# The written order of 1233 steps, the loads' order and the places of the tiles, all drawn up anew

## The chip, the cores and the metric

The program runs on one core of a Trainium2 chip. The metric is device time in microseconds (us): 275.06 us before, the median of three runs (273.14, 275.06 and 277.61).

## What is computed

A column-normalised attention, whose output is the input of a soft mixture of experts; B, N, C are 4, 5056, 256 and there are 32 slots.

```python
def _attn_ref(q, k, v, tau):                 # per batch
    qn = q / (np.linalg.norm(q, axis=1, keepdims=True) + 1e-06)
    kn = k / (np.linalg.norm(k, axis=1, keepdims=True) + 1e-06)
    s = kn.transpose(0, 2, 1) @ qn / tau     # 256 x 256
    a = softmax(s)
    return v @ a

def _moe_ref(x, phi, w1, w2):                # x: all rows of all batches
    logits = x @ phi                         # 20224 x 32
    slot_input = softmax(logits, axis 0).T @ x
    slot_out = per expert: np.maximum(slot_input[e] @ w1[e], 0.0) @ w2[e]
    return softmax(logits, axis 1) @ slot_out
```

## The kernel before

**Tiles.** Inputs come in tiles of 1 MiB (128 partitions by 2048 fp32), each one DMA on SP's queue. There are 40 tiles q0 to q39 (ten for each batch; each holds four pieces of q and k side by side), 20 tiles v0 to v19, nine tiles x4 to x12 (v transposed by the host), eight w1 tiles and eight w2 tiles. The output leaves in 21 stores. All these tiles and the large intermediates live in 23 places of 1 MiB. `SLOTS` says which place each takes; a load into a place waits for the last reader of the tile that was there before. `BANKS` does the same for the eight PSUM banks.

**Stages.** For each q tile: `cast` (L356, ScalarE) makes the high half of a split pair, `low` (L360, GpSimd, 117 of them) the low half, `square` (L370, ScalarE) the squares, `add` (L388, VectorE) sums them, and `score` (L408, TensorE) multiplies each piece into S, either the split pair or the raw fp32 tile. After the ten tiles of a batch comes a chain that ends in M, the attention matrix times phi: `att_cols` (L444, TensorE), `att_rn` (L449, VectorE), `att_pow` (L454, GpSimd, a square root), `att_norm` (L458 ScalarE, L459 VectorE), `att_row` (L471, TensorE), `att_scale`, `att_exp`, `att_turn`, `att_phi` (L511). With M, each v tile gives `logits` (L566, TensorE; needs v transposed: from an x tile, or by `turn`, L546, and a copy, L551), then exponentials, and `gather` (L666, TensorE). After the last, `gather(19)`, come `finish` steps, the experts (`up` L810, `flip_h` L828, `down` L843, `o_fold` L859), and 29 `out_mul` steps (L878 for half blocks of 512 rows by 128 columns of output, L893 for whole blocks). Each `out_mul` is copied out of PSUM by four `out_evict` (L906, ScalarE and VectorE in turn) and stored by SP (L911). On the side, GpSimd does `c_sub` and `c_mul` (L764, L779) for the softmax over the slots.

**What sets the order.** `plan` lists 1233 steps by name. `run` executes them in the order of `ORDER`, a list of their numbers, and so every engine, SP's queue included, gets its own steps in the order in which they stand there; each engine works in order, and semaphores make it wait for data and for places. No planner runs: the order, the places and the banks are written out.

Of the kernel before, what the change touches and what calls it, by code (L numbers as in the profile page):

```python
# [58 lines left out]
    901, 10, 9, 0, 11, 1, 903, 34, 33, 12, 42, 17, 20, 35, 900, 902, 30, 21, 22, 899, 897, 898, 2, 15, 26,  # L59
    904, 27, 19, 8, 18, 41, 39, 29, 14, 16, 45, 46, 50, 36, 23, 28, 51, 24, 38, 905, 13, 58, 57, 907, 54, 5,  # L60
    43, 47, 7, 32, 82, 48, 56, 6, 906, 81, 912, 61, 60, 59, 70, 908, 909, 83, 914, 84, 87, 65, 89, 44, 69,
    31, 145, 77, 91, 85, 25, 49, 147, 92, 93, 78, 90, 76, 64, 3, 72, 71, 148, 73, 62, 75, 74, 80, 910, 95,
    149, 96, 86, 94, 911, 105, 106, 63, 4, 146, 37, 66, 55, 99, 40, 97, 110, 111, 88, 917, 79, 155, 156, 53,
    102, 173, 915, 120, 174, 52, 98, 100, 113, 124, 107, 150, 157, 895, 913, 115, 104, 68, 158, 109, 151,
    112, 118, 131, 67, 132, 133, 108, 103, 176, 177, 153, 134, 117, 183, 101, 135, 121, 821, 119, 916, 114,
    126, 140, 152, 154, 141, 123, 825, 826, 942, 896, 918, 125, 217, 175, 221, 189, 116, 122, 824, 823, 127,
    185, 184, 130, 143, 142, 827, 828, 216, 829, 128, 830, 834, 211, 136, 178, 220, 219, 222, 203, 187, 223,
    137, 160, 225, 129, 197, 186, 831, 224, 201, 215, 159, 182, 190, 194, 572, 227, 568, 198, 163, 205, 231,
    919, 162, 920, 213, 161, 832, 835, 169, 179, 239, 228, 208, 921, 171, 924, 244, 164, 922, 196, 207, 180,
    138, 237, 218, 139, 168, 170, 566, 570, 204, 212, 236, 167, 248, 188, 202, 206, 172, 144, 191, 192, 247,  # L70
    837, 229, 571, 226, 166, 210, 238, 245, 567, 230, 243, 569, 234, 255, 214, 278, 292, 235, 181, 258, 254,
    193, 232, 165, 320, 264, 200, 249, 233, 310, 199, 314, 312, 250, 246, 209, 256, 240, 573, 836, 284, 833,
    241, 925, 242, 923, 306, 252, 195, 311, 838, 253, 282, 324, 298, 263, 259, 260, 313, 265, 322, 839, 840,
    262, 290, 316, 317, 842, 841, 941, 319, 285, 251, 268, 257, 560, 554, 321, 266, 315, 926, 940, 542, 548,
    561, 318, 327, 293, 555, 546, 270, 543, 843, 305, 549, 288, 844, 291, 556, 289, 335, 960, 271, 558, 544,
    269, 279, 547, 261, 557, 545, 574, 286, 577, 302, 340, 550, 927, 929, 845, 559, 562, 267, 273, 272, 846,
    275, 576, 353, 551, 294, 326, 552, 323, 564, 930, 303, 344, 345, 347, 283, 848, 334, 847, 575, 296, 280,
    281, 354, 352, 356, 578, 277, 579, 553, 852, 600, 849, 332, 359, 304, 853, 339, 850, 563, 338, 357, 365,
    287, 928, 299, 297, 307, 348, 355, 346, 580, 276, 565, 274, 343, 341, 342, 943, 588, 362, 854, 962, 376,
    590, 295, 591, 934, 360, 361, 301, 300, 368, 581, 372, 364, 350, 851, 931, 380, 383, 381, 385, 384, 363,  # L80
    367, 371, 856, 349, 589, 333, 582, 366, 351, 594, 358, 592, 369, 330, 331, 370, 584, 933, 585, 593, 382,
    595, 374, 325, 586, 603, 596, 602, 599, 386, 411, 329, 985, 309, 393, 857, 328, 986, 855, 440, 377, 858,
    583, 587, 932, 961, 373, 396, 378, 375, 387, 390, 598, 604, 388, 379, 389, 445, 400, 401, 337, 336, 308,
    618, 601, 397, 417, 937, 402, 439, 605, 861, 597, 425, 620, 862, 863, 444, 391, 392, 621, 606, 965, 419,
    944, 501, 607, 608, 442, 407, 394, 622, 859, 426, 508, 418, 408, 430, 623, 453, 452, 443, 404, 946, 963,
    403, 626, 624, 619, 611, 628, 629, 433, 860, 625, 438, 612, 455, 964, 441, 938, 448, 409, 459, 460, 641,
    645, 630, 609, 613, 434, 631, 451, 395, 450, 412, 644, 424, 428, 436, 627, 864, 866, 429, 935, 865, 515,
    632, 520, 635, 432, 431, 614, 420, 449, 945, 870, 437, 633, 947, 954, 519, 410, 415, 528, 468, 527, 471,
    514, 615, 634, 647, 642, 987, 646, 399, 637, 500, 516, 638, 639, 867, 416, 616, 871, 447, 643, 427, 446,
    640, 953, 507, 617, 699, 705, 936, 456, 648, 414, 422, 467, 649, 706, 509, 988, 505, 464, 523, 504, 518,  # L90
    650, 872, 398, 868, 423, 435, 406, 513, 512, 454, 458, 457, 869, 526, 405, 651, 461, 522, 478, 477, 463,
    484, 958, 966, 939, 486, 493, 494, 476, 701, 691, 465, 873, 700, 783, 692, 487, 495, 967, 874, 413, 875,
    703, 876, 968, 704, 462, 499, 466, 517, 525, 421, 777, 469, 610, 636, 956, 778, 502, 689, 473, 488, 503,
    654, 652, 479, 492, 491, 530, 702, 529, 779, 532, 510, 781, 524, 668, 782, 531, 784, 521, 664, 780, 996,
    672, 496, 666, 667, 511, 485, 538, 742, 949, 539, 534, 470, 675, 506, 690, 738, 533, 541, 540, 948, 955,
    475, 489, 481, 743, 687, 670, 674, 676, 536, 535, 653, 673, 740, 669, 688, 537, 665, 472, 693, 483, 741,
    671, 694, 879, 880, 881, 490, 677, 678, 959, 655, 882, 679, 989, 656, 657, 480, 732, 730, 739, 497, 731,
    658, 733, 728, 729, 660, 498, 661, 474, 482, 795, 789, 878, 659, 883, 884, 877, 888, 885, 680, 997, 990,
    950, 796, 993, 992, 998, 957, 951, 726, 793, 727, 707, 662, 695, 886, 790, 681, 683, 684, 952, 889, 891,
    999, 890, 794, 709, 697, 711, 887, 744, 752, 753, 892, 893, 682, 745, 663, 1000, 894, 754, 756, 755,  # L100
    791, 712, 792, 710, 713, 696, 750, 751, 734, 708, 698, 736, 757, 785, 788, 746, 748, 758, 714, 715, 760,
    716, 747, 717, 721, 797, 762, 799, 763, 735, 759, 764, 769, 765, 685, 718, 719, 787, 801, 1001, 995,
    770, 800, 766, 773, 686, 767, 771, 772, 720, 749, 768, 786, 802, 803, 722, 798, 774, 775, 723, 969, 724,
    804, 805, 976, 806, 761, 807, 1007, 725, 810, 811, 808, 809, 776, 812, 814, 815, 813, 816, 819, 975,
    973, 974, 820, 737, 817, 1008, 1018, 818, 1009, 1019, 1037, 991, 1010, 972, 970, 971, 1029, 1030, 1048,
    1011, 1049, 978, 977, 980, 1038, 1056, 994, 1002, 1031, 1032, 1057, 1050, 1012, 1058, 1039, 1051, 1020,
    1059, 1033, 1034, 1005, 1003, 1040, 1006, 1021, 1004, 1035, 1036, 979, 1041, 1042, 1043, 1044, 1045,
    1022, 982, 984, 981, 1023, 1016, 1013, 1046, 1047, 1087, 1090, 1015, 1088, 1127, 1089, 1128, 1132, 1133,
    1091, 1135, 1129, 1131, 983, 1134, 1136, 1077, 1130, 1080, 1081, 1067, 1069, 1220, 1071, 1078, 1082,
    1083, 1052, 1053, 1084, 1085, 1070, 1079, 1072, 1054, 1055, 1060, 1061, 1086, 1076, 1068, 1073, 1027,  # L110
    1074, 1122, 1124, 1075, 1126, 1062, 1063, 1064, 1117, 1065, 1119, 1121, 1218, 1125, 1123, 1118, 1120,
    1066, 1107, 1109, 1108, 1214, 1212, 1112, 1116, 1111, 1110, 1115, 1114, 1113, 1162, 1165, 1163, 1216,
    1164, 1221, 1177, 1166, 1202, 1179, 1180, 1205, 1178, 1204, 1203, 1223, 1102, 1181, 1104, 1014, 1142,
    1144, 1146, 1206, 1226, 1106, 1105, 1103, 1145, 1147, 1151, 1148, 1150, 1215, 1025, 1137, 1140, 1143,
    1026, 1139, 1141, 1092, 1094, 1024, 1138, 1217, 1095, 1231, 1096, 1167, 1171, 1168, 1170, 1169, 1197,
    1198, 1200, 1199, 1201, 1157, 1230, 1149, 1160, 1187, 1188, 1224, 1189, 1190, 1191, 1161, 1192, 1193,
    1017, 1028, 1196, 1195, 1159, 1172, 1174, 1194, 1175, 1228, 1176, 1173, 1225, 822, 1182, 1229, 1183,
    1184, 1207, 1208, 1210, 1211, 1158, 1097, 1222, 1099, 1100, 1098, 1209, 1152, 1155, 1153, 1154, 1156,
    1219, 1232, 1093, 1186, 1101, 1185, 1227, 1213,
]  # L120
SLOTS = {
    "q0": 6, "q1": 0, "q2": 7, "q3": 3, "q4": 11, "q5": 12, "q6": 15, "q7": 13, "q8": 17, "q9": 18,
    "q10": 20, "q11": 21, "q12": 16, "q13": 0, "q14": 19, "q15": 12, "q16": 10, "q17": 22, "q18": 16,
# [1019 lines left out]
```

## Time and profile before

| | |
|---|---|
| median of three runs | 275.06 us (273.14 to 277.61) |
| the profiled execution's own time | 276.03 us |
| its span, first to last instruction | 274.3 us |
| moved by DMA | 109.73 MB, of it 88.38 MB read and 20.97 MB written by the kernel's own loads and stores |
| busy: TensorE (PE), VectorE, ScalarE, GpSimd (POOL) | 250.7, 207.8, 206.9, 170.2 us |
| mean granted TensorE clock | 0.96 |

How to read it: busy shares are shares of the span. The page cuts the span into 40 slices of 6.86 us and gives a digit (tenths busy) for each engine and the GB/s moved. "Idle before" is the time an engine stood still before an instruction, with what ended it.

### The profile page before, as it was taken

How to read it: one execution, taken by the hardware profiler on the slowest of the kernel's cores; microseconds unless marked ns; L12 is line 12 of the kernel's file. 1: busy time of each engine (PE TensorE's matmuls, PEld its weight loads, DVE VectorE, ACT ScalarE, POOL GpSimd, SP SyncE). 2: the span in 40 equal slices, each digit the busy share in tenths (PEclk: the TensorE clock that was granted, in tenths of full speed). 3: DMA queues.
4: the chain of work that ended last, by engine and by line, in shares of the span. 5: the costliest groups of instructions: out<-in, count | busy, mean ns of one | idle time of the engine just before them, and what ended most of it. 6: DMA issues, size and time to landing. Idle time of an engine off the chain costs nothing.

```text
span 274.3 us, 5939 instructions
## 1 busy us (share of the span) xinstructions
PE 250.7 (91%) x2272; PEld 197.2 (72%) x2272; DVE 207.8 (76%) x416; ACT 206.9 (75%) x325; POOL 170.2 (62%) x135
## 2 busy tenths in 40 slices
PE   5799999999999999999989999999999899999800
PEld 5688888888898778776758977976545767767500
DVE  1068998599998999889979987799957756965410
ACT  3999999899999999999998793665837445653500
POOL 1776999999999989999998797903054300000000
PEclk9999999999999999999999999999999999996755
DMA  7999999999998999999999999999999997999995
GB/s 276 417 421 418 424 422 420 410 424 422 412 418 337 375 362 361 424 422 419 418 412 421 415 384 403 424 423 421 417 421 418 394 415 326 415 416 421 409 405 244
DMA packets 16013, 109.73 MB, mean 400 GB/s; under 512 B 1905, under 2 KB 1905, under 8 KB 3569
## 3 DMA queue, kind: packets, MB, share of 16 engines
q1 hardware_dynamic: 15984, 109.36, 97.5%
q8 instruction: 18, 0.29, 0.4%
q14 instruction: 11, 0.08, 0.1%
HBM read 88.38 MB, written 20.97 MB: 399 GB/s over the span
## 4 chain that ended last, share of the span: by engine, by line
PE 84%; DMA 7%; issue 2%; ACT 2%; DVE 1%; DVEq 0%; SPq 0%; ACTq 0%
PE S L408 42%; PE T L546 7%; PE L L566 6%; PE G L666 6%; PE op L878 6%; PE op_None L893 5%; DMA arena<-in_one_dram 4%; PE O L843 3%; DMA q<-in_one_dram 3%; PE H L810 3%; PE Mp L511 1%; PE S L426 1%; PE hTp L828 1%; PE aTp L499 1%; PE wake L324 1%
## 5 line engine op out<-in xcount | busy, mean ns | idle before, releaser
L360 POOL TENSOR_TENSOR hl<-arena,hl 128x512 fp32r<-128x512 f32 x98 | 123.6, 1303 | 9.8 <-ACT hl L356 7.2
L408 PE MATMUL S<-hl 128*128 128x512 f32 x468 | 97.4, 353 | 0.0
L408 PEld LDWEIGHTS S<-hl 128*128 128x128 f32 x468 | 73.3, 190 | 12.0 <-issue 2.1
L388 DVE TENSOR_TENSOR A<-sq,A 128x512 f32<-128x512 f32 (+1 forms) x68 | 45.6, 688 | 14.9 <-ACT A L369 12.7
L356 ACT CAST hl<-arena 128x1024 fp32r<-128x1024 f32 (+1 forms) x58 | 51.3, 911 | 2.0 <-PE S L408 1.9
L388 DVE TENSOR_TENSOR A<-arena,A 128x512 f32<-128x512 f32 (+1 forms) x76 | 51.0, 690 | 1.7 <-ACT arena L370 0.5
L370 ACT ACTIVATE arena<-arena 128x2048 f32<-128x2048 f32 (+1 forms) x17 | 30.7, 1812 | 0.7 <-ACT arena L370 0.3
L360 POOL TENSOR_TENSOR hl<-q,hl 128x512 fp32r<-128x512 f32 x19 | 24.1, 1289 | 7.5 <-ACT hl L356 7.5
L370 ACT ACTIVATE sq<-arena 128x2048 f32<-128x2048 f32 (+2 forms) x15 | 27.4, 1831 | 0.6 <-ACT rk L465 0.5
L408 PE MATMUL S<-arena 128*128 128x256 f32 x108 | 26.5, 380 | 0.0
L408 PEld LDWEIGHTS S<-arena 128*128 128x128 f32 x108 | 19.3, 189 | 2.8 <-issue 0.3
L546 PE MATMUL T<-ident,arena 128*128 128x128 f32 x140 | 19.3, 274 | 0.8 <-DMA arena<-in_one_dram 0.8
L878 PE MATMUL op<-cT,so 32*128 32x256 f32 x144 | 17.2, 423 | 1.4 <-ACT so L865 0.8
L546 PEld LDWEIGHTS T<-ident,arena 128*128 128x128 f32 x140 | 16.1, 142 | 2.1 <-DVE acc L719 1.2
L408 PE MATMUL S<-q 128*128 128x256 f32 x48 | 13.5, 424 | 3.6 <-DMA q<-in_one_dram 3.6
L878 PEld LDWEIGHTS op<-cT,so 32*128 32x128 f32 x144 | 11.6, 183 | 5.4 <-ACT arena L906 1.4
L779 POOL TENSOR_TENSOR nat<-nat,cs 128x1280 f32<-128x1280 f32 x3 | 7.0, 2347 | 12.9 <-DVE cs L776 12.9
L906 ACT COPY oh<-op 128x256 f32<-128x256 f32 x28 | 9.0, 380 | 7.9 <-PE op L878 7.7
L666 PE MATMUL G<-arena,dn 128*32 128x256 f32 x232 | 14.8, 382 | 0.0
L906 DVE COPY oh<-op 128x256 f32<-128x256 f32 x28 | 10.8, 418 | 4.9 <-PE op L878 2.4
L408 PEld LDWEIGHTS S<-q 128*128 128x128 f32 x48 | 9.8, 216 | 5.4 <-issue 3.9
L893 PE MATMUL op_None<-so,cT 32*128 32x256 f32 x96 | 11.6, 470 | 0.2
(164 smaller groups left out, 413.3 us busy)
## 6 DMA issues: line engine op xcount, KB each, us to landing
arena<-in_one_dram SPq DMA_DIRECT2D x59, 1024.0 KB, 11.6
w<-in_one_dram SPq DMA_DIRECT2D x7, 1024.0 KB, 19.7
out_dram<-arena SPq DMA_DIRECT2D x7, 1024.0 KB, 7.1
q<-in_one_dram SPq DMA_DIRECT2D x6, 1024.0 KB, 8.2
out_dram<-oh SPq DMA_DIRECT2D x6, 1024.0 KB, 5.7
out_dram<-o SPq DMA_DIRECT2D x6, 1024.0 KB, 7.8
v<-in_one_dram SPq DMA_DIRECT2D x5, 1024.0 KB, 11.2
arena<-in_one_dram SPq DMA_DIRECT2D x4, 896.0 KB, 10.3
```

Of the source, the lines that this page charges most:

```text
L356: act.copy(parts(u, lo, hi)[:, :, 0::2, :], raw(u)[:, lo:hi])
L360: pool.tensor_tensor(hl[:, :, 1::2, :], raw(u)[:, lo:hi], hl[:, :, 0::2, :].bitcast(F32), op=ALU.subtract)
L370: act.activation(sq(u)[:, n : NQ[u]], raw(u)[:, n : NQ[u]], AF.Square)
L388: dve.tensor_tensor(a[r], s[r, j], a[r], op=ALU.add)
L408: pe.matmul(S_[:, lo:hi], l, r, start=first, stop=False, skip_group_check=True)
L546: pe.transpose(tp[:, P * jj : P * jj + P], vtile(p, 4 * h + jj)[:, P * m : P * m + P], ident)
L566: pe.matmul(L[S * g : S * g + S, :n, :], M[:, m, :], x[:, :n, S * g : S * g + S], start=m == 0 and g not in void, stop=m == 1, skip_group_ ...
L666: pe.matmul(gp[S * g : S * g + S, :C], dn[:, x, j, :], vtile(p, j), start=x == 0 and j < G, stop=x == n - 1 and j >= G,)
L810: pe.matmul(hp[S * g : S * g + S, :], slT[:, d, :], w1t(G * r + g)[:, d, x * UT : x * UT + UT], start=d == 0, stop=d == 1,)
L878: pe.matmul(ops[b, p, hf, g], so[r, hf], cT[b][r, 8 * p : 8 * p + 8, :].rearrange("s j t -> s (j t)"), start=True, stop=True,)
L893: pe.matmul(ops[b, p, hf, g][:, h, :], cT[b][r, 4 * i : 4 * i + 4, :].rearrange("s j t -> s (j t)"), rhs[r], start=True, stop=True,)
L906: (dve.tensor_copy if g % 2 else act.copy)(dst, ops[b, p, hf, g])
```

## The change

Three lists are replaced: `ORDER`, `SLOTS` and `BANKS`. Steps, tile sizes, loads, stores, the split of work between engines, and all functions stay. The first line of the old and the new `ORDER`, in each the line with step 881 (`att_pow(3)`), and the first line of `SLOTS`; 490 is the `low` of q36's last piece, 990 is `c_mul(0)`:

```diff
-    901, 10, 9, 0, 11, 1, 903, 34, 33, 12, 42, 17, 20, 35, 900, 902, 30, 21, 22, 899, 897, 898, 2, 15, 26,
...
-    671, 694, 879, 880, 881, 490, 677, 678, 959, 655, 882, 679, 989, 656, 657, 480, 732, 730, 739, 497, 731,
...
+    901, 0, 821, 1, 902, 9, 12, 903, 11, 10, 900, 899, 898, 21, 24, 17, 18, 897, 20, 30, 22, 904, 33, 34,
...
+    877, 880, 777, 781, 778, 672, 674, 990, 957, 659, 881, 882, 655, 656, 657, 883, 676, 740, 658, 687, 660,
...
 SLOTS = {
-    "q0": 6, "q1": 0, "q2": 7, "q3": 3, "q4": 11, "q5": 12, "q6": 15, "q7": 13, "q8": 17, "q9": 18,
...
+    "q0": 5, "q1": 0, "q2": 1, "q3": 3, "q4": 7, "q5": 10, "q6": 15, "q7": 12, "q8": 17, "q9": 18,
...
```

With the numbers turned into names, these are the places that the prediction speaks of:

| | before | after |
|---|---|---|
| first loads | q1, q3, a quarter of q0, q2, three quarters of q0, q4 | q1, q2, q3, four quarters of q0, q4 |
| first on ScalarE | square(1), cast(1), square(3), cast(3) | cast(1), square(1), cast(2), square(2) |
| first `score` on TensorE | of q3, then of q1 | of q1 three times, then of q2 |
| end of `low` on GpSimd | ..., att_pow(3), low(36), low(35), c_sub(1), c_mul(0) | ..., low(39), low(36), c_mul(0), att_pow(3), c_sub(1) |
| steps of TensorE from att_row(3) to gather(19) | 22.4 us of work in the trace | the same and peak_row(2,0), six more turn steps, two fewer |
| last loads | w1 tiles, then w2 tiles | w1 and w2 tiles mixed, three w1 tiles late among them |
| out_mul, first nine | those of column half 0, with `down` of half 1 between them | the same set in nearly the same order |
| out_mul, the rest | half blocks and whole blocks mixed; (2,2), (2,4), (3,4), (0,1), (1,3) last | whole blocks (2,2), (2,3), (2,1), (3,1), (2,0) first; (0,0), (1,2), (1,0), (0,2), (3,3) last |
| 12th to 15th store | o3_2, o2_1, o3_0, o2_2 | o3_2, o3_0, o2_4, o3_4 |

## Rows read from the trace of the kernel before

**Rows 1.** The page: busy time and instructions of each engine; DMA queue: packets, MB, share.
```profile
PE 250.7 (91%) x2272; PEld 197.2 (72%) x2272; DVE 207.8 (76%) x416; ACT 206.9 (75%) x325; POOL 170.2 (62%) x135
...
q1 hardware_dynamic: 15984, 109.36, 97.5%
```

**Rows 2.** Busy time by stretch: us, PE, PEld, DVE, ACT, POOL, clock, DMA share, GB/s.
```profile
0.00:5.50 5.50, 3.78 (x16) 3.48 (x16) 1.13 (x11) 1.28 (x1) 0.71 (x6) 1.00 0.67 246
5.50:82.00 76.50, 73.57 (x393) 64.40 (x393) 60.30 (x98) 74.44 (x75) 67.69 (x55) 1.00 1.01 418
82.00:110.00 28.00, 28.00 (x249) 22.70 (x251) 26.11 (x50) 27.42 (x41) 27.16 (x22) 1.00 0.95 360
110.00:150.00 40.00, 39.20 (x366) 28.97 (x355) 35.41 (x73) 38.52 (x53) 38.11 (x31) 1.00 1.01 419
150.00:175.00 25.00, 25.00 (x226) 21.02 (x226) 20.86 (x41) 17.86 (x36) 21.50 (x18) 1.00 1.01 406
175.00:216.00 41.00, 39.87 (x581) 26.18 (x579) 33.45 (x80) 23.84 (x62) 12.83 (x7) 1.00 1.01 420
216.00:230.00 14.00, 12.45 (x220) 9.08 (x221) 8.49 (x25) 6.72 (x23) 2.16 (x1) 1.00 0.88 362
230.00:245.00 15.00, 14.53 (x151) 11.59 (x151) 12.12 (x27) 9.37 (x22) 0.00 (x0) 1.00 1.01 414
245.00:262.00 17.00, 14.28 (x92) 9.80 (x87) 9.93 (x18) 7.43 (x16) 0.00 (x0) 0.71 0.99 407
262.00:274.30 12.30, 0.00 (x0) 0.00 (x0) 0.00 (x0) 0.00 (x0) 0.00 (x0) 0.50 0.78 323
```

**Rows 3.** Waits of SP's queue from 62 to 125 us: total us, times, longest.
```profile
SPq L264 <- POOL hl L360: 25.3, 10, 5.2
```

**Rows 4.** Timeline of the start, by engine (start, us, instruction, idle before).
```profile
5.55 1.91 ACT L370 ACTIVATE sq<-q 128x2048 f32<-128x2048 f32 x1 [3.54 <-DMA q<-in_one_dram]
7.37 1.03 ACT L356 CAST hl<-q 128x1024 fp32r<-128x1024 f32 x1
...
8.43 3.75 PE L408 MATMUL S<-q 128*128 128x256 f32 x8 [3.60 <-DMA q<-in_one_dram]
...
8.48 2.50 POOL L360 TENSOR_TENSOR hl<-q,hl 128x512 fp32r<-128x512 f32 x2 [7.17 <-ACT hl L356]
...
18.02 2.53 POOL L360 TENSOR_TENSOR hl<-arena,hl 128x512 fp32r<-128x512 f32 x2 [1.71 <-ACT hl L356]
```

**Rows 5.** Timeline at the end of the last batch's attention, by engine.
```profile
170.14 1.01 POOL L454 TENSOR_TENSOR rn<-rn,half 128x4 f32<-128x4 f32 x1 [1.63 <-DVE rn L449]
171.12 2.52 POOL L360 TENSOR_TENSOR hl<-arena,hl 128x512 fp32r<-128x512 f32 x2
...
175.91 2.35 POOL L779 TENSOR_TENSOR nat<-nat,cs 128x1280 f32<-128x1280 f32 x1
...
171.51 0.18 DVE L459 RECIPROCAL rn<-rn 128x4 f32<-128x4 f32 x1 [1.00 <-ACT rn L458]
...
176.56 0.38 PE L471 MATMUL rq<-ident,rn 128*128 128x128 f32 x2
```

**Rows 6.** Chain that ended last: start, us, what.
```profile
57.59 0.44 PE T L546 x4
...
175.85 0.87 PE T L546 x8
176.72 0.22 PE rq L471 x2
...
199.45 0.49 DVE gs L681
```

**Rows 7.** SP's queue: the last load issued, the first and the last stores.
```profile
200.85 0.33 SPq L264 DMA_DIRECT2D arena<-in_one_dram  x1
217.89 4.23 SPq L911 DMA_DIRECT2D out_dram<-oh  x3
...
262.44 1.21 SPq L911 DMA_DIRECT2D out_dram<-oh  x1
```

**Rows 8.** TensorE's timeline in the output stage.
```profile
229.77 2.32 PE L893 MATMUL op_None<-so,cT 32*128 32x256 f32 x31
...
251.85 2.21 PE L893 MATMUL op_None<-so,cT 32*128 32x256 f32 x16
```

240 rows, old and new, of tables (BANKS, ORDER, SLOTS) are left out of this document.

## Prediction

> **What bounds the kernel now.** I read the page first, then the table of busy time by stretch, then the waits of SP's queue, the timelines of the start and of the end of the attention, and the chain.
>
> The page shows two resources near their limit at once: the DMA queue has its 16 engines busy 97.5% of the span, TensorE 91% [rows 1]. The table by stretch says where [rows 2]. A full stretch moves 418 to 422 GB/s. At 422, the 109.73 MB of the execution would take 260.0 us, against a span of 274.3: 14.3 us are lost. Each stretch loses its length times (1 - rate/422): 2.3 us in the first 5.5 us, 0.7 up to 82 us, 4.1 from 82 to 110 (360 GB/s), 0.3 up to 150, 0.9 up to 175, 0.2 up to 216, 2.0 from 216 to 230 (362 GB/s), 0.3 and 0.6 up to 262, and 2.9 in the last 12.3 us. The first and the last term are the wait for the first byte and the closing of the last transfers, which any order has. So an order can give back at most the other 9.1 us.
>
> TensorE has nothing to give back in the middle: 28.00 busy of 28.00 us, 39.20 of 40, 25.00 of 25 [rows 2]. GpSimd is as full in the attention: 27.16 of 28.00 us from 82 to 110, 38.11 of 40 from 110 to 150 [rows 2]. The three limits hang together: in the weak stretch SP's queue waits for places in the large pool, most of all for GpSimd's `low` (25.3 us in ten waits) [rows 3], and `low` waits for loads. The time is thus a balance of three nearly full lines, and reordering moves no work off any of them.
>
> **The change part by part.** The sum is made against the profiled execution, 276.03 us, which lies 0.97 above the median of 275.06.
>
> *The start.* TensorE's first score now needs q1 alone. It waited 3.60 us for q3, until 8.43; q1 was there when ScalarE began its squares, at 5.55 [rows 4]. So TensorE can begin 2.9 us earlier. The next steps cover themselves: two raw scores of q1 take some 3.75 us, as the first eight matmuls did [rows 4]; the third needs a `low`, and with the cast (1.03) ahead of the squares (1.91) GpSimd begins near 6.6 instead of 8.48 [rows 4]. For GpSimd that lead is soon lost, for it then waits for q4, as it did at 18.02 [rows 4], and the same 4 MiB are still ahead of q4. The `constants` step now comes first on ScalarE and costs it nothing, since ScalarE waits for q1 anyway. Term: 0 for the loads and GpSimd; for TensorE between -2.9 and 0, by whether something else holds it later.
>
> *The places of the loads.* No load may start before the last readers of its place are through. I laid each engine's steps in the new order end to end, each with its duration in this trace, set the end of each place's last reader beside the moment at which an unbroken transfer (2.48 us for a MiB at 422 GB/s) would want the place, and did the same for the old order. Old: 22 of 72 loads late, the worst by 3.2 us (v15, behind a `low`). New: 18 of 71, the worst by 3.2 us (v14, behind logits(9)). Lateness against an unbroken transfer doesn't add up, its maximum counts; so the term is 0. Bounds: -4.1 if the weak stretch from 82 to 110 closed altogether, +4.1 if a second one like it opened [rows 2].
>
> *The end of the attention.* Old: GpSimd does att_pow(3) at 170.14, then the last two `low` until 173.64 [rows 5]. New: all `low` first, then c_mul(0), 2.35 us, then the power, 1.01 [rows 5]. Queued behind the power are, on ScalarE and VectorE, the two parts of att_norm(3), and on TensorE att_row(3) with all its steps up to gather(19). Without the power the `low` end 1.0 earlier, near 172.6; if GpSimd works through its wait of 1.63 us as well [rows 5], at 171.0. The power then ends at 174.4 to 176.0. From its end to the end of the reciprocal it took 0.54 us (171.15 to 171.69) [rows 5], so att_row(3) can start at 175.0 to 176.6; it started at 176.56 [rows 5]. Behind att_row(3) stood 22.4 us of TensorE work up to gather(19) (176.94 to 199.36) [rows 6]; now there is a peak_row of 0.1 and a net four turns of 0.44 more, 24.3 in all. So gather(19) ends between 199.4 and 201.0 where it ended at 199.3, a cost of 0 to 1.6 if GpSimd is what holds TensorE there; if it isn't, TensorE's lead of 2.9 from the start comes through. Other waits of TensorE on late `low` (of q39, q36 and q35, whose scores stand up to 3.4 us ahead of them in the new order by the same laying out) lie in front of this one and are covered by it. Bounds -2.9 and +1.6; I take 0, which is nearest to the rows of GpSimd, the fuller line here.
>
> *Late w1 tiles.* Three of them now come among the w2 tiles, some 5 us later than before. `up` of their half is moved behind the other half, and they would still land 3 us ahead of it. Term 0; it becomes 1 or 2 if TensorE comes with its full lead.
>
> *The stores.* The chain from gather(19) to the first store is step for step the same, and took 18.6 us (199.3 to 217.89) [rows 6, 7]. The last load was issued at 200.85 [rows 7], with seven more ahead of it at 2.48 us each, so loads end near 220.6. The stores then need 20.97 MB / 422 = 49.7 us, to 270.3; 2.0 and 0.6 are lost on the way because outputs weren't ready [rows 2], and the last landing is near 273. In the new order the worst readiness is that of the 14th store, o2_4: by old durations 11.0 us behind an unbroken transfer, against 9.1 for the worst before, oh1_1_1. But the old durations carry the fall of the granted clock to half: 2.21 us for a whole block at 251.85, against 2.32 for two blocks at 229.77 [rows 8]. Five steps that stood there, (2,2), (3,0), (3,1), (0,1) and (1,3), now come ahead of (2,4) and earlier, which takes some 3.5 us off that lateness (an estimate, at some 0.7 each). So between 1.9 later and 1.6 earlier (11.0 and 7.5 against 9.1). I take 0, between the two.
>
> Sum: 276.03 + 0, or 275.1 on the scale of the median. All terms stand at zero for the same reason: the order changes which line is short of slack, not how full the lines are.
>
> **One rule against one row.** Rows: TensorE's matmuls fill every stretch from 82 to 175 us but for 0.8 us, its weight loads only 22.70 of 28.00 [rows 2]. The Trainium skill ("Trainium Kernel Development and Optimization", Best Practices) calls matmul busy time a bad measure of the distance to the limit and would have weight loads read instead; by that TensorE would be 72% full [rows 1] and could take up several us of waits unseen. That would lower the chance of the slower rival below to about 0.05 and leave the sum at 275.1. The trace speaks against it here: four matmuls of a turn take 0.44 us at 57.59 and eight take 0.87 at 175.85 [rows 6], so the matmuls run at one fixed pace and there is no slack inside the busy time.
>
> **The rivals.**
>
> *The gaps close.* TensorE keeps its 2.9 us, the weak stretch of the transfers (4.1) closes in part, and outputs come early enough to close the 2.0 at 216 to 230. For it: the new order has fewer late loads (18 against 22) and an earlier start. Against it: the worst lateness is the same, and outputs cannot come earlier than TensorE. Price: 2.9 + 2.0 + half of 4.1 = 7.0, so 268.1.
>
> *TensorE is made to wait at the end of the attention.* Place: scores of q39, q36, q35, then att_row(3), all behind GpSimd. It decides if GpSimd is later than in the old trace, for instance because the loads of q36 or q39 slip. Price: the largest lateness of a score (3.4) no longer covered but ahead of the power and c_mul (3.4 together, less the 1.6 already weighed): 3.4 + 1.8, and the lateness of the 14th store (1.9), together 7.1 with the unchanged rest: 282.2. For it: TensorE has no slack to take a wait back. Against it: GpSimd's work is the same, and its waits from 82 to 150 us were only 2.7 us [rows 2].
>
> *The clock falls sooner.* In the old trace the stretch from 245 on has a mean granted clock of 0.71 [rows 2]. If pauses in the output stage make it fall at 230, whole blocks take some 2.2 us instead of 1.2 [rows 8]; that is still below the 2.48 us of their store, so at most 1 or 2 us: 277.
>
> **How the numbers follow.** No change of note, 275.1: 0.66; its own range is 275.1 - 2.9 - 1.6 = 270.6 to 275.1 + 1.6 + 1.9 = 278.6. Gaps close: 0.13. TensorE waits: 0.15. Clock: 0.06. The range is 270.5 to 280.0: it holds the first case, the clock, and the cheaper part of the slower rival. A measurement of this kernel can tell a change of 2%, 5.5 us, from none; the lines are 269.6 and 280.6. Of the fast rival 0.10 lies beyond the line, of the slow one 0.12: faster 0.10, same 0.78, slower 0.12.
>
> **What would show it.** Right: DMA share still near 97%; TensorE's first score near 5.6; a stretch of weak transfers between 80 and 150 us again; att_row(3) within 2 us of 176.6 and released by ScalarE or GpSimd; first store within 2 us of 217.9. Wrong: TensorE idle for more than 3 us in sum between 150 and 200; a first store before 215 or after 221; transfers above 410 GB/s all through.

## The result and the profile after

The changed kernel takes 272.58 us (median of 20 runs, 270.55 to 274.68), the kernel before 276.15 beside it (20 runs, 273.14 to 278.83): a ratio of 0.9899 with a 95% interval of 0.987 to 0.9929. It is nearer to 1 than the ratio of these medians, 0.987, because executions over 1.5% above the fastest of their kernel are left out of it, here and in all ratios below. That lies within 2% and inside the range forecast, but it is no "no change": the kernel is faster by 1%, some 2.8 us.

The profiled execution took 272.60 us (span 270.8), 3.4 less than that of before. The page of the changed kernel, busy time and DMA queue, against [rows 1]:

```profile
PE 248.1 (92%) x2272; PEld 197.0 (73%) x2272; DVE 207.4 (77%) x416; ACT 205.8 (76%) x325; POOL 169.7 (63%) x135
...
q1 hardware_dynamic: 15984, 109.36, 98.2%
```

The queue's share is 0.7 points higher. The table of busy time by stretch of the changed kernel, against [rows 2]:

```profile
0.00:5.50 5.50, 4.21 (x18) 3.91 (x18) 1.13 (x11) 1.49 (x2) 0.70 (x6) 1.00 0.65 234
5.50:82.00 76.50, 75.93 (x414) 65.42 (x414) 59.51 (x97) 75.13 (x80) 69.56 (x56) 1.00 1.02 419
82.00:110.00 28.00, 28.00 (x271) 22.94 (x267) 26.96 (x53) 27.77 (x41) 28.00 (x24) 1.00 0.97 378
110.00:150.00 40.00, 39.83 (x352) 31.94 (x344) 37.04 (x75) 39.44 (x52) 39.79 (x32) 1.00 1.01 418
150.00:175.00 25.00, 25.00 (x243) 20.20 (x245) 21.41 (x43) 16.60 (x34) 19.96 (x15) 1.00 1.02 421
...
216.00:230.00 14.00, 13.28 (x244) 10.45 (x243) 11.63 (x31) 8.17 (x22) 2.35 (x1) 1.00 1.00 415
230.00:245.00 15.00, 13.97 (x138) 9.93 (x134) 11.06 (x24) 8.57 (x22) 0.00 (x0) 1.00 1.01 421
245.00:262.00 17.00, 8.49 (x46) 6.57 (x46) 6.30 (x14) 4.50 (x12) 0.00 (x0) 0.53 1.01 421
```

The weak stretch from 82 to 110 us is still there (378 GB/s, was 360), the one from 216 to 230 is nearly gone (415, was 362). The start in the changed kernel's timeline, against [rows 4]:

```profile
5.68 1.04 ACT L356 CAST hl<-q 128x1024 fp32r<-128x1024 f32 x1 [3.45 <-DMA q<-in_one_dram]
5.79 3.75 PE L408 MATMUL S<-q 128*128 128x256 f32 x8 [0.53 <-DMA q<-in_one_dram]
...
24.03 1.05 PE L408 MATMUL S<-hl 128*128 128x512 f32 x4
...
124.65 1.93 PE L566 MATMUL L<-arena,M 128*32 128x256 f32 x32 [0.17 <-DMA arena<-in_one_dram]
...
6.80 2.50 POOL L360 TENSOR_TENSOR hl<-q,hl 128x512 fp32r<-128x512 f32 x2 [5.50 <-ACT hl L356]
...
17.93 1.29 POOL L360 TENSOR_TENSOR hl<-q,hl 128x512 fp32r<-128x512 f32 x1 [1.59 <-ACT hl L356]
```

TensorE begins at 5.79 instead of 8.43. The rows at 24.03 and 124.65 are score(1,0) and logits(6), which waits 0.17 us for its load, tile x6; both are needed below. GpSimd's earlier start is gone by q4: 17.93, was 18.02. The end of the attention, against [rows 5]:

```profile
159.53 5.04 POOL L360 TENSOR_TENSOR hl<-arena,hl 128x512 fp32r<-128x512 f32 x4
164.51 2.37 POOL L779 TENSOR_TENSOR nat<-nat,cs 128x1280 f32<-128x1280 f32 x1
168.04 1.01 POOL L454 TENSOR_TENSOR rn<-rn,half 128x4 f32<-128x4 f32 x1 [1.17 <-DVE rn L449]
...
169.41 0.18 DVE L459 RECIPROCAL rn<-rn 128x4 f32<-128x4 f32 x1 [0.83 <-ACT rn L458]
...
171.33 0.38 PE L471 MATMUL rq<-ident,rn 128*128 128x128 f32 x2
```

The last `low` ends near 164.6, not 173.6. `c_mul(0)`, ahead of the power, cost nothing: behind it the power still waited 1.17 us for VectorE. And att_row(3) shows no idle time: the reciprocal ended at 169.6, TensorE came 1.7 us later, because it was still at work. From there to the stores, timelines of TensorE and SP's queue:

```profile
196.75 0.63 PE L691 MATMUL gt<-fold,gs 128*128 128x32 f32 x4 [0.69 <-DVE gs L681]
...
198.47 0.33 SPq L264 DMA_DIRECT2D arena<-in_one_dram  x1
214.65 0.35 SPq L911 DMA_DIRECT2D out_dram<-oh  x1
...
256.72 1.19 SPq L911 DMA_DIRECT2D out_dram<-o  x1
```

The row at 196.75 is `finish_fold(3)`, 0.69 us behind the end of gather(19); I use its start as the mark of TensorE's progress in all runs. Before, it stood at 199.99, right behind the gs step of [rows 6] (199.45 + 0.49), 3.2 us later, and TensorE had waited once on the way, for the load of v14:

```profile
142.39 0.96 PE L546 MATMUL T<-ident,arena 128*128 128x128 f32 x7 [0.76 <-DMA arena<-in_one_dram]
...
199.99 0.63 PE L691 MATMUL gt<-fold,gs 128*128 128x32 f32 x4 [0.69 <-DVE gs L681]
```

The first store is 3.24 earlier, too (214.65, was 217.89). The last load lands at 218.85 (was 220.61), 1.76 earlier; from there the stores take 50.7 us (was 52.3; 49.7 is their floor at 422 GB/s).

So TensorE is earlier by what it gained at its start, 8.43 - 5.79 = 2.64; by 0.3 of waits (0.76 us for v14 before, 0.28 and 0.17 us in two places after); and by 0.2 because `wake(1,8)`, two matmuls of 0.11 us that stood at 45.1 us, now comes ahead of the first score. GpSimd's waits for casts shrank with it, in the view of waits from 20 to 170 us. Before:

```profile
POOL hl L360 <- ACT hl L356: 5.5, 8, 1.9
```

After:

```profile
POOL hl L360 <- ACT hl L356: 1.5, 1, 1.5
```

GpSimd, which I had taken for the leading engine, had been waiting for ScalarE's casts. Of ScalarE's own waits ahead of casts, 1.3 us were for tiles that TensorE's scores had yet to free (0.3 after); what held the casts otherwise isn't shown.

### The profile page after: what moved, and what is told of

Read it like the earlier page. It is cut to its first block, busy times and chain, and to the rows that moved or that the text cites. A ratio compares the mean times of both kernels' runs of the same rounds, so it can differ in the third digit from the quotient of the medians.

```text
span 270.8 us, 5935 instructions
## 1 busy us (share of the span) xinstructions
PE 248.1 (92%) x2272; PEld 197.0 (73%) x2272; DVE 207.4 (77%) x416; ACT 205.8 (76%) x325; POOL 169.7 (63%) x135
## 5 line engine op out<-in xcount | busy, mean ns | idle before, releaser
L360 POOL TENSOR_TENSOR hl<-arena,hl 128x512 fp32r<-128x512 f32 x103 | 129.2, 1311 | 2.2 <-ACT hl L356 1.5
L408 PE MATMUL S<-hl 128*128 128x512 f32 x468 | 96.7, 352 | 0.3 <-POOL hl L360 0.3
L408 PEld LDWEIGHTS S<-hl 128*128 128x128 f32 x468 | 73.1, 190 | 11.4 <-issue 1.2
L388 DVE TENSOR_TENSOR A<-arena,A 128x512 f32<-128x512 f32 (+1 forms) x102 | 67.8, 688 | 4.4 <-ACT arena L370 2.5
L370 ACT ACTIVATE arena<-arena 128x2048 f32<-128x2048 f32 (+2 forms) x25 | 44.2, 1776 | 0.0
L388 DVE TENSOR_TENSOR A<-sq,A 128x512 f32<-128x512 f32 x42 | 28.2, 690 | 14.2 <-ACT A L369 13.2
L408 PE MATMUL S<-arena 128*128 128x256 f32 x100 | 24.8, 380 | 0.0
L360 POOL TENSOR_TENSOR hl<-q,hl 128x512 fp32r<-128x512 f32 x14 | 17.8, 1288 | 9.1 <-ACT hl L356 9.1
L878 PE MATMUL op<-cT,so 32*128 32x256 f32 x144 | 20.2, 465 | 1.2 <-ACT arena L906 0.5
L408 PEld LDWEIGHTS S<-arena 128*128 128x128 f32 x100 | 17.7, 189 | 2.7 <-DMA arena<-in_one_dram 0.4
L408 PE MATMUL S<-q 128*128 128x256 f32 x56 | 14.9, 418 | 0.5 <-DMA q<-in_one_dram 0.5
L370 ACT ACTIVATE sq<-arena 128x2048 f32<-128x2048 f32 x8 | 15.4, 1919 | 0.0
L566 PE MATMUL L<-arena,M 128*32 128x256 f32 (+1 forms) x224 | 14.3, 380 | 0.2 <-DMA arena<-in_one_dram 0.2
L764 POOL TENSOR_TENSOR arena<-arena,cm 128x1280 f32<-128x1280 f32 x2 | 4.7, 2346 | 14.0 <-DVE cm L761 14.0
L408 PEld LDWEIGHTS S<-q 128*128 128x128 f32 x56 | 11.3, 210 | 2.5 <-PE wake L324 0.8
L589 ACT COPY lt<-L 128x256 f32<-128x256 f32 x20 | 7.2, 369 | 5.8 <-DVE dn L648 3.2
```

The lines of the kernel that those rows point to most:

```text
L360: pool.tensor_tensor(hl[:, :, 1::2, :], raw(u)[:, lo:hi], hl[:, :, 0::2, :].bitcast(F32), op=ALU.subtract)
L370: act.activation(sq(u)[:, n : NQ[u]], raw(u)[:, n : NQ[u]], AF.Square)
L388: dve.tensor_tensor(a[r], s[r, j], a[r], op=ALU.add)
L408: pe.matmul(S_[:, lo:hi], l, r, start=first, stop=False, skip_group_check=True)
L566: pe.matmul(L[S * g : S * g + S, :n, :], M[:, m, :], x[:, :n, S * g : S * g + S], start=m == 0 and g not in void, stop=m == 1, skip_group_ ...
L589: act.copy(lts[b, gi][:, x], Ls[p].rearrange("p j s -> p (j s)"))
```

## The experiments

The kernels below have their lists printed in longer lines, so their line numbers are 12 lower: L396 is `score` (L408), L312 `wake`, L679 `finish_fold`. Fifteen kernels ran; the ratio is always to the kernel before, run beside it on the same chip. "Lead" is the theory that TensorE's earlier start passes through to the end.

**More wake steps on the changed kernel (e1, e2).** A `wake` step is two matmuls on constants; the edit was meant to hold TensorE back.

```diff
-WAKES = ((-8, 8),)
+WAKES = ((-8, 15),)
```

> The changed kernel with 15 instead of 8 rounds of the dummy matmuls ahead of TensorE's first score; nothing else differs. They end near 8.4 us instead of 5.3, so the first score comes near 8.4 instead of 5.8, where it was before the change. Theory of the lead (TensorE works without a pause from its first score to the last gather, so a later start comes out whole at the end): 1.5 to 2.7 us over the changed kernel's 272.6, about 274 to 275.3, a ratio to the kernel before of 0.995 to 0.999 (the lower end if the warmer clock speeds up the first scores). Rival (the places and the transfers decide, TensorE's start is covered): 272.6 to 273, ratio 0.990.

> The changed kernel with 22 rounds of dummy matmuls: first score near 11.7 us, some 6 us late. Theory of the lead: 4.8 to 6 us over the changed kernel, 277.4 to 278.6, ratio 1.006 to 1.010. Rival (places and transfers decide): under 274, ratio under 0.994.

Measured: 15 steps 272.54 us, ratio 0.9903 (0.9865 to 0.9941), as the changed kernel; 22 steps 274.62, ratio 0.9984 (0.9946 to 1.0022). That looked like the fall of the lead theory, until TensorE's timeline with 15 steps was read:

```profile
1.05 5.60 PE L312 MATMUL wake<-ones 128*128 128x128 f32 x32 [1.05 <-DVE ones L298]
6.71 1.99 PE L396 MATMUL S<-q 128*128 128x256 f32 x8
...
22.86 1.05 PE L396 MATMUL S<-hl 128*128 128x512 f32 x4
...
124.70 1.93 PE L554 MATMUL L<-arena,M 128*32 128x256 f32 x32 [0.76 <-DMA arena<-in_one_dram]
```

The same eight matmuls that took 3.75 us at 5.79 took 1.99 here. Two stretches of the table for the changed kernel, then for this one:

```profile
7.00:8.50 1.50, 1.50 (x5) 1.14 (x5) 0.00 (x0) 1.50 (x2) 1.50 (x2) 1.00 1.01 426
8.50:10.00 1.50, 1.50 (x6) 1.22 (x5) 0.00 (x0) 1.31 (x3) 1.25 (x2) 1.00 0.96 403
```

```profile
7.00:8.50 1.50, 1.50 (x9) 1.32 (x8) 0.00 (x0) 1.50 (x2) 1.50 (x2) 1.00 1.02 426
8.50:10.00 1.50, 1.50 (x9) 1.31 (x9) 0.00 (x0) 1.50 (x3) 1.28 (x2) 1.00 0.97 406
```

Nine matmuls in 1.5 us instead of five or six. TensorE started 0.9 us later and was 1.2 ahead by score(1,0) (22.86 against 24.03); with 22 steps it was level (24.13). So neither run delayed TensorE, and `finish_fold(3)` stood at 196.76 and 197.12. The experiment didn't do what it was made for, but it shows a limit of the lead: the 1.2 us that TensorE was ahead with 15 steps were gone by `finish_fold(3)` (196.75 in the changed kernel). Some 0.6 of them went at logits(6), where it waited 0.76 us for x6 instead of 0.17, since x6 landed at the same time (124.57 and 124.51). What made 22 steps slower lies behind gather(19), in its table by stretch:

```profile
195.00:200.00 5.00, 4.31 (x46) 3.39 (x38) 3.29 (x11) 2.96 (x10) 0.00 (x0) 0.89 1.02 418
200.00:205.00 5.00, 5.00 (x25) 1.18 (x28) 3.08 (x6) 0.98 (x2) 2.34 (x1) 0.50 1.02 424
...
215.00:220.00 5.00, 4.16 (x64) 3.25 (x55) 4.17 (x10) 2.53 (x9) 0.00 (x0) 1.00 0.54 213
```

The granted clock fell to half in the experts, the first store came at 218.33 instead of 214.65, and the queue starved (213 GB/s). With 15 steps the clock fell there, too, for a shorter time, and the first store came at 216.37.

**The new start in the old order (e3).**

```diff
-score(3,3), score(1,2), score(1,1) / square(1), cast(1), constants
+score(1,2), score(1,3), score(3,3), score(1,1) / constants, cast(1), square(1)
```

> The kernel before with the new start alone: TensorE's first two scores are those of q1, whose raw pieces need no low half, ahead of the score of q3; the cast of q1 comes ahead of its squares. The order of loads, the places and all the rest are as before. TensorE starts near 5.7 instead of 8.4. Theory of the lead: the gain appears here too, 2 to 2.7 us, ratio 0.990 to 0.993. Rival (the middle's order and the places made the gain): no change, ratio 0.998 to 1.002.

Measured: 274.06, ratio 0.9979 (0.9936 to 1.0023): not told apart from none. In its profile `finish_fold(3)` stands at 197.68 and the loads end at 218.51, both 2 us earlier than before, and this one execution took 273.30 us, 2.7 less than the profiled one of before. But the median misses what the lead theory expected, 0.990 to 0.993, and falls where its rival had put it: a lead of TensorE at 198 us didn't become time here, and why not stays open.

**Two quarters of q0 ahead of q1, five wake steps (e4).**

```diff
-load q1, q2, q3, quarters of q0 / score(1,2), score(1,3)
+load two quarters of q0, q1, q2, q3, two quarters / score(0,3), score(0,2), score(1,2)
```

> The changed kernel with two quarters of q0 (256 KiB each) loaded ahead of q1, the raw scores of these quarters first on TensorE, and 5 rounds of dummy matmuls instead of 8. TensorE can start near 3.9 instead of 5.8; q1 comes some 1.3 us later. Theory of the lead: 1 to 1.9 us under the changed kernel, 270.7 to 271.6, ratio 0.980 to 0.984. Rival (the start is covered): 272.6 or up to 0.6 more for the later q1, ratio 0.990 to 0.992.

Measured: 276.44, ratio 1.0028 (0.9992 to 1.0064). The scores of q0 ran early, but q1 came later and TensorE then stood 3.59 us for it; `finish_fold(3)` at 200.04. All of the change's gain was gone with TensorE's lead, though its order was in place; the clock fell for some us near 203 us as well.

**The outputs' order exchanged (e5, e6, e10), and a control (e11).** From `o_back(0)` on, one kernel with the order of the other; the output tiles' places and banks had to be assigned anew, by a rule (the one free longest).

```diff
-out_mul, out_evict, store and c_ steps in the kernel's own order
+the same steps in the other kernel's order
```

> The changed kernel up to its first o_back step, from there the order of the kernel before (outputs, evictions, stores). Theory TensorE-line: TensorE works without a pause from its first score to gather(19), so what it saves early arrives whole at gather(19) and at the first store; the order of the outputs is worth nothing. It expects gather(19) at 196.1 us, a first store near 214.7 and a median near 272.6 (ratio 0.990). Theory output-order: the gain is that whole blocks come first, so that no output is late. It expects gather(19) at 196.1 too, but weak transfers (below 390 GB/s) between 216 and 230 us and a median of 274 to 275 (ratio 0.997 or more).

> The kernel before up to its first o_back step, from there the changed order of the outputs. TensorE-line: gather(19) stays at 197.5 to 199.3 us, median 275 (ratio 0.998 to 1.0). Output-order: the same gather(19), transfers above 410 GB/s between 216 and 230 us, median 272.6 to 273.5 (ratio 0.990 to 0.995).

> Again the changed kernel with the outputs in the old order from its first o_back step on, but now the c_ steps (VectorE's transposes for the softmax over the slots, ScalarE's and GpSimd's parts) stay where the changed kernel has them, so that VectorE isn't held by c_mul(3) ahead of the first outputs. gather(19) near 196.0 in all theories. If the order of the outputs is worth little: loads end near 218.9, the stores take 51 to 51.5 us behind them, median 272.5 to 273.5 (ratio 0.990 to 0.993). If it carries the gain: stores 52 to 53 us, median 274 to 275 (ratio 0.994 to 0.998).

> Control for the kernels with exchanged output orders: the changed kernel in its own order throughout, with the places and PSUM banks of its output tiles assigned by the same rule as there (the place or bank that has been free longest). If the rule is neutral: median 272.6 (ratio 0.990). If the written places matter: 273.5 or more, and the exchanged orders above have to be read against this one.

Measured: changed kernel with the old outputs 289.87 (1.0538, 1.0496 to 1.058), in the second form 283.73 (1.0274, 1.022 to 1.0327); kernel before with the new outputs 279.14 (1.0128, 1.0091 to 1.0166); the control 275.17 (0.9952, 0.9907 to 0.9996). The first three lie far outside what either theory expected. The control alone is at 0.9952 where the changed kernel is at 0.9899, some 1.5 us, though these two intervals overlap; so the grafts can't tell what an order is worth. They do show waits for banks. TensorE's costliest group from 212 us on, idle time last, in the control

```profile
L866 PE MATMUL op<-cT,so 32*128 32x256 f32 x144 | 16.5, 449 | 4.6 <-DVE arena L894 2.8 <-ACT arena L894 1.4 <-ACT so L853 0.4
```

and in the changed kernel

```profile
L878 PE MATMUL op<-cT,so 32*128 32x256 f32 x144 | 20.2, 465 | 1.2 <-ACT arena L906 0.5 <-ACT so L865 0.4 <-ACT o L906 0.2
```

The same steps in the same order wait 4.6 us instead of 1.2, mostly for evictions, with other banks and places. The control's clock also fell near 200 us (0.90 and 0.76 in the stretches from 195 to 200 and to 205), so the time that it lost isn't due to the banks alone as far as is shown.

**TensorE alone 3 us later (e8).** Now with the pace known: 26 matmuls behind score(1,0).

```diff
-LATE = (1, 3)
+LATE = (13, 3)
-wake(1,8) near the head of the order
+wake(1,8) behind score(1,0)
```

> The changed kernel with 26 more matmuls of the wake kind (0.112 us each at the full pace) on TensorE behind score(1,0), at 25 us: TensorE alone is 2.9 us later, nothing else is touched. TensorE-line: gather(19) near 199.0 us, first store near 217.5, loads end 1 to 2 us later, median 275 (ratio about 1.0). Rival, GpSimd and the places of the loads set the pace and TensorE regains its lateness in its waits for them: gather(19) at 196.1 to 196.6, median 272.6 (ratio 0.990).

Measured: 275.15, ratio 0.9961 (0.9925 to 0.9997). Its timelines of TensorE and SP:

```profile
24.68 3.06 PE L312 MATMUL wake<-ones 128*128 128x128 f32 x26
27.57 1.03 PE L396 MATMUL S<-arena 128*128 128x256 f32 x4
...
200.19 0.63 PE L679 MATMUL gt<-fold,gs 128*128 128x32 f32 x4 [0.69 <-DVE gs L669]
...
218.09 0.35 SPq L899 DMA_DIRECT2D out_dram<-oh  x1
```

The score behind the added matmuls comes at 27.57 instead of 24.92, 2.65 us later (score(1,0) itself came 0.24 earlier than in the changed kernel), and `finish_fold(3)` 3.44 later. Nothing was regained on the way; 0.65 came on top at logits(6), which waited 0.82 us for x6 instead of 0.17. In time it is 0.6% by the ratios, 1.7 us, with intervals that just touch (2.6 between the medians, each beside runs of its own of the kernel before). The loads end at 222.07, 3.2 later. With TensorE late, places come free late: from 5 to 82 us SP's queue waited 20.6 us in all for TensorE's scores, 18.8 in the changed kernel. The table shows it at once:

```profile
5.50:82.00 76.50, 75.93 (x415) 66.30 (x416) 57.07 (x93) 72.95 (x76) 66.88 (x54) 1.00 1.00 402
```

402 GB/s where the changed kernel has 419. In the changed order TensorE's lateness passes through, as the lead theory says. Of a lead added to it that isn't always so: with 15 wake steps it was gone, with 13 and a filling (below) it was kept.

**The old order with TensorE warm (e9).**

```diff
-WAKES = ((-8, 8),)
+WAKES = ((-8, 24),)
```

> The kernel before with 24 wake steps instead of 8, so that TensorE has no pause before its first score at 8.4 us. Runs with 15 and 22 wake steps on the changed kernel showed the first eight matmuls at 1.99 us instead of 3.75. TensorE-line: first eight in 1.99 us, score(1,0) 1.8 us earlier, gather(19) 1.5 to 1.8 us earlier than in the profile of before, median 273.5 to 274.2 (ratio 0.994 to 0.997). Rival as above: no change of gather(19), median 275.1 (ratio 1.0).

Measured: 273.39, ratio 0.9936 (0.9907 to 0.9965), with not one step of the order changed. Its timeline of TensorE:

```profile
9.27 1.99 PE L396 MATMUL S<-q 128*128 128x256 f32 x8
...
198.30 0.63 PE L679 MATMUL gt<-fold,gs 128*128 128x32 f32 x4 [0.69 <-DVE gs L669]
```

It is 1.7 us earlier than before at `finish_fold(3)`, and about 1.8 us in time (0.0064 of 276.31).

**Filling TensorE's wait behind gather(19) (e12, e13).**

```diff
-LATE = (1, 3)
+LATE = (3, 3)
-wake(1,8) early in the order
+wake(1,8) right behind gather(19)
```

> The kernel before with six more matmuls of the wake kind on TensorE right behind gather(19), where TensorE waits 0.69 us for VectorE; nothing else is touched. In several profiles the granted clock fell to half for 3 to 8 us around 200 us. Theory pause: that fall is brought on by TensorE's pauses behind gather(19), and costs the kernel before some 3 us in about half of its executions. It expects no fall between 195 and 210 us and a median near 274 with few executions above 276 (ratio 0.993 to 0.997). Rival: the fall doesn't hang on that pause: median 275 to 276 with the same spread (ratio 1.0).

> The changed kernel with the same six filling matmuls behind gather(19) (its first wake step, which stood at the start, is taken for it). Theory pause: no fall between 195 and 210 us, median 271.7 to 272.2 (ratio 0.985 to 0.988), as the changed kernel is less sensitive to it, its first store being 4 us ahead of the end of the loads. Rival: 272.6 (ratio 0.990).

Measured: before with the filling 274.07, ratio 0.993 (0.9895 to 0.9964); changed kernel with it 271.92, ratio 0.9841 (0.9791 to 0.9892). Two stretches of the latter, against those of the run with 22 wake steps:

```profile
195.00:200.00 5.00, 5.00 (x58) 4.09 (x56) 3.47 (x11) 3.33 (x13) 0.00 (x0) 1.00 1.02 421
200.00:205.00 5.00, 5.00 (x49) 1.59 (x52) 3.07 (x6) 2.37 (x5) 2.35 (x1) 1.00 1.02 419
```

Of the twelve profiles without the filling (both kernels and ten experiments) seven show the clock at half for some us between 195 and 210; of the five with it (these two and the next three), none. The seven aren't spread evenly: of the six profiles without the filling in which the matmuls had reached their full pace by 6.7 us, all six fell, of the other six one; with the filling, none of three and none of two. One of the five fell at 234 us instead (e16). On the kernel before the filling gains 0.7%; on the changed kernel the intervals with and without it overlap. That the 0.7% are what the falls cost isn't shown: neither this profile nor that of before has a fall near 200, yet TensorE is 1.0 us ahead at `finish_fold(3)`, since it didn't wait for v14 (0.76) and `wake(1,8)` (0.22) had left its place at 45 us. And of the twelve executions with the filling five had a mean clock of 0.941 to 0.949 and took 274.7 to 276.3 us; the other seven had 0.956 or more and took at most 274.15.

**Both causes apart (e14, e15, e16).** All with the filling, and

```diff
-WAKES = ((-8, 8),)
+WAKES = ((-8, 13),)   in the changed kernel, first run
+WAKES = ((-8, 36),)   in the changed kernel, second run
+WAKES = ((-8, 24),)   in the kernel before
```

> The changed kernel with 13 wake steps at the start, so that TensorE has no pause before q1 lands, and with the six filling matmuls behind gather(19). First eight matmuls 2.0 us instead of 3.75, score(1,0) near 22.4 us. If TensorE's lead still passes through: gather(19) 1.5 us earlier, median 270.7 (ratio 0.981). If it is used up where logits(6) waits for its x tile (0.69 to 0.76 us at 124 us in the runs with 15 wake steps and with the filling): gather(19) at 196.0 to 196.6, median 271.8 to 272.2 (ratio 0.984 to 0.987), as with the filling alone.

> The changed kernel with 36 wake steps at the start, which end near 11 us at the full pace, and with the filling: TensorE is about 2.9 us later than in the changed kernel, from the start on, and the clock is held behind gather(19). gather(19) near 198.5 to 199.3, as in the kernel before with the filling (198.3). If the start is the whole of the gain: the median of that kernel, 274.1 (ratio 0.993). If the new order of the outputs and the places give something by themselves: 273.0 to 273.5 (ratio 0.988 to 0.991). If TensorE's lateness is regained in its waits: 272 (ratio 0.985).

> The kernel before with 24 wake steps and the filling: TensorE's first scores at the full pace and the clock held behind gather(19), in the old order. If both causes are the gain of the change and add: gather(19) near 197.2, median 272.5 to 273 (ratio 0.986 to 0.990), what the changed kernel has. If the gain hangs on the new order: 274 (ratio 0.993).

Measured: 271.56, ratio 0.984 (0.9794 to 0.9886); 276.61, ratio 1.0032 (1.0 to 1.0065); 273.13, ratio 0.9896 (0.9846 to 0.9946). TensorE's timeline in the second of them, the changed order without its lead:

```profile
12.08 1.99 PE L396 MATMUL S<-q 128*128 128x256 f32 x8
...
201.70 0.62 PE L679 MATMUL gt<-fold,gs 128*128 128x32 f32 x4
```

and in the third, the old order with the lead:

```profile
8.70 1.99 PE L396 MATMUL S<-q 128*128 128x256 f32 x8
...
197.74 0.62 PE L679 MATMUL gt<-fold,gs 128*128 128x32 f32 x4
```

The old order with a TensorE at full pace from its first scores and with the filling has what the change gave (0.9896 against 0.9899). The new order without the lead, 1.7 us behind the kernel before at `finish_fold(3)`, has none of it; 1.0032 is clear of the 0.9841 and 0.984 with the lead. At an equal mark (197.61 and 197.74, both with the filling) the new order has 0.9841 and the old 0.9896; these intervals overlap. (I expected TensorE 2.9 us late in the second; it was 4.1 at score(1,0), since the steps reached 12 us, not 11.) The first is 1.3 us ahead of the changed kernel with the filling at score(1,0) (22.71 against 24.03) and 1.44 at `finish_fold(3)` (196.17 against 197.61), though it waits 0.56 us for a load at logits(6); its time isn't told apart from 0.9841.

All runs by TensorE's progress, without the four with exchanged outputs or banks:

| kernel | finish_fold(3) at, us | loads end, us | median, us | ratio |
|---|---|---|---|---|
| changed, 13 wakes, filling | 196.17 | 218.27 | 271.56 | 0.984 |
| changed | 196.75 | 218.85 | 272.58 | 0.9899 |
| changed, 15 wakes | 196.76 | 218.91 | 272.54 | 0.9903 |
| changed, 22 wakes | 197.12 | 219.25 | 274.62 | 0.9984 |
| changed, filling | 197.61 | 219.03 | 271.92 | 0.9841 |
| before, new start | 197.68 | 218.51 | 274.06 | 0.9979 |
| before, 24 wakes, filling | 197.74 | 219.09 | 273.13 | 0.9896 |
| before, 24 wakes | 198.30 | 219.04 | 273.39 | 0.9936 |
| before, filling | 198.97 | 219.74 | 274.07 | 0.993 |
| before | 199.99 | 220.61 | 275.1 to 276.7 | 1 |
| changed, q0 first | 200.04 | 222.22 | 276.44 | 1.0028 |
| changed, TensorE late | 200.19 | 222.07 | 275.15 | 0.9961 |
| changed, 36 wakes, filling | 201.70 | 223.77 | 276.61 | 1.0032 |

From the first row to the last TensorE is 5.5 us later and the median 5.1. Each mark is from one profile, and the rows aren't in strict order of the ratio: two with a mark below 198, 22 wakes (with a fall of the clock) and before with the new start, are near 1.

## Why the prediction was wrong, step by step

**The balance.** "A balance of three nearly full lines" was where it went wrong: the lines aren't equal. Up to gather(19) a later TensorE is later throughout: a full TensorE can't regain what it lost at the start, and GpSimd had waits to give up (5.5 us to 1.5). A lead beyond that of the change can meet a load that isn't there yet: with 15 wake steps it was used up.

**The start: the failed step.** I bounded it by -2.9 and 0, and the sum took 0, because GpSimd was to hold TensorE at the end of the attention. TensorE's first score came 2.64 us earlier and `finish_fold(3)` 3.2, and holding TensorE back by about as much cost 0.6% (e8), some 1.7 of the 2.8 us that the change gained. The bound was right, the choice in it wrong, and the rows for choosing stood in [rows 2]: TensorE had 28.00 of 28.00, 39.20 of 40, 25.00 of 25 us. I read "nothing to give back" as "no gain"; it means that what it starts earlier it ends earlier, as long as its loads are there. That a lead at 198 us becomes time in the old order as well is shown by 24 wake steps (0.9936), not by the new start (0.9979).

**The end of the attention.** I took GpSimd to hold TensorE there. [rows 5] said otherwise: the reciprocal was over at 171.69 and att_row(3) came at 176.56 without any idle time ahead of it, so TensorE, not GpSimd, was 4.9 us late. After the change it is 1.7 late. The price of `c_mul(0)` ahead of the power, 0 to 1.6, was 0. (By its own terms the sum should have said 0.3 to 1.9: it leaves out the 0.38 us of att_row(3) itself. The 24.3 us behind it were right: from 171.71 to 196.06.)

**The places of the loads.** By themselves near the forecast: the weak stretch stayed, 378 GB/s. But the end of the loads isn't apart from TensorE, as I had it: it moved by 1.76 with the change and by 3.2 the other way when TensorE alone was held back. At an equal TensorE (e8 against before, 200.19 and 199.99) the new places end the loads 1.5 us later (222.07 against 220.61, one profile each); over the whole table the loads end 21.4 to 22.2 us behind `finish_fold(3)` in the changed order, 20.6 to 21.4 in the old.

**The stores.** Taken 0 between -1.6 and +1.9; measured -1.6 in the profile, and the feared 14th store, o2_4, was issued at 243.8 with the queue at 421 GB/s. The five steps that come earlier aren't needed to explain it. In these profiles the stores lose least where the first of them is ready long before the loads end: 4.2 us ahead in the changed kernel (loss 1.0 against the floor), 2.7 before (2.6), 1.1 with 24 wakes (3.3). The old order, with 3.5 us ahead (e16), lost 0.9. At equal TensorE the new order's stores took 50.4 us (e8) against 52.3, which pays for its later loads. What the order of outputs gives alone stays open within some 0.4% (e8).

**Late w1 tiles.** No wait of `up` was seen, as forecast, with TensorE 3 us ahead.

**The rule against the row.** The Trainium skill ("Trainium Kernel Development and Optimization", Best Practices) would have read the weight loads, 72 to 73% here, as room in TensorE. By that, as the prediction worked it out, several us of waits would have been taken up unseen; TensorE 2.65 us late at 27.57 was 3.44 late at 200 (e8). The row was right on that. My own sentence, that matmuls run at one fixed pace, was not: at the start the same eight take 3.75 or 1.99 us.

**The rivals.** "Gaps close" had the direction and the mechanism at 0.13, and was too large (268.1): it added the lead (2.9) and the gaps (2.0 and 2.05). The gap at 216 to 230 us nearly closed, the one at 82 to 110 by 18 GB/s; whether they close because of the lead isn't shown apart from it. "TensorE waits" didn't occur: its idle time from 150 to 175 us is nil. "The clock falls sooner" was seen in variants of both kernels, mostly near 200 us and once at 234 (e16), not in the profiles of the two kernels themselves.

**What would show it.** One of the three signs of being wrong came: a first store before 215 (214.65). Transfers above 410 GB/s all through did not, the weak stretch stayed, and TensorE wasn't idle for 3 us between 150 and 200. Of the signs of being right two failed: att_row(3) came 5.3 us earlier than 176.6 and no engine released it, and the first store was 3.24 us early.

## What to carry to other kernels

Where one engine shows no idle time over most of the span, its first instruction is part of the critical path: a start 2.6 us earlier was still there 190 us later, whatever the other engines' busy shares, up to the point where a load came too late for it. Longer warm-up and six filling matmuls, in the old order, gave as much as a new order of 1233 steps (0.9896 against 0.9899); a first operand that is there first gave TensorE its lead, but no gain that could be told from none (0.9979). Before an engine is called the one that holds another, look for the idle time in front of the held instruction: where there is none, nothing held it. And a delay put in on purpose must be seen in the trace to be one; here two such runs raised the pace of TensorE's first matmuls.

## What the runs showed of the hardware

**TensorE's pace at the start.** With the granted clock shown as 1.00, the upper of its levels (2.4 GHz), the first raw matmuls still ran at half pace: 0.427 us from start to start where TensorE had paused 0.53 us (changed kernel) or 3.60 us (before) after its wake steps, and until about 10.4 and 13.3 us. Where it had worked without a pause since 1.05 us (13 to 36 wake steps) they ran at 0.216 us from the second on; the wake matmuls went from 0.213 to 0.112 us at 4.4 to 6.7 us, at another moment in each run. Once at the full pace it was kept over a pause of 3.59 us (q0 first: the eight matmuls behind it took 1.99). The pause alone doesn't decide it. The control e11 begins with the very steps of the changed kernel, and its eight came behind a pause of 1.03 us:

```profile
5.95 1.97 PE L396 MATMUL S<-q 128*128 128x256 f32 x8 [1.03 <-DMA q<-in_one_dram]
```

Its wake matmuls had reached 0.112 us at 4.5 us, ahead of the pause. With the same start the eight took 1.97 us in e5, too, and 3.75 in e10: an equal start ran at either pace in different executions. Longer warm-up is what had the full pace ready for the first score in every run that had it (six of six). In these traces the list of granted clocks begins at just these moments (10.38 us in the changed kernel, 13.29 before, 4.78 with 15 wake steps, 4.42 in e11); the 1.00 ahead of them stands for no entry. The Trainium skill ("TensorE: Matmul & The Clock Gate", Part 1) says that the array starts at 1.2 GHz and that activity releases it. The paces agree with that; the granted clock in the views doesn't show it.

**The clock behind gather(19).** A wait of 0.69 us and some small matmuls stood ahead of falls to 0.50 in seven of twelve profiles; six matmuls in that wait and none of five profiles had one. That the wait brings the fall on is likely by these counts, not shown one by one: five profiles without the filling kept 1.00 over the same wait, and the falls went with an early rise of the pace at the start (six of seven).

**PSUM banks.** The same output order with another assignment of banks and places made TensorE's costliest group wait 4.6 us instead of 1.2; what it cost in time (0.9952 against 0.9899) isn't clear of the noise, and that run's clock fell near 200 us.
